# Seven products for eight in the first matmul of the last two batches, of attention and a Silu MoE layer on one core

## The chip, the core and the metric

The kernel runs on 1 core of one Trainium2 chip. The metric is the device time of one execution, in microseconds (us). The engines: TensorE (PE, matmuls, with its weight loads as PEld), VectorE (DVE), ScalarE (ACT), GpSimd (POOL) and SyncE (SP); the last two issue DMAs here, POOL the loads and SP the stores.

## What is computed

Attention over q, k, v of (8 batches, 12 heads, 448 tokens, 64), then a dense layer with Silu over the 3584 tokens x 768:

```
scores = matmul(q, k.T) / sqrt(64);  attn = softmax(scores);  a = matmul(attn, v)
x = a.transpose(0, 2, 1, 3).reshape(3584, 768)
h = x @ w_in                       # 768 x 2048
g = h * (1.0 / (1.0 + exp(-h)))
out = g @ w_out                    # 2048 x 768, float32
```

## The kernel before, in words

All tiles are fp16 with fp32 sums. `w_in_t` (128 partitions, 6 chunks of 128 rows, 2048) and `w_out_t` stay in SBUF.

*Attention.* A unit is a batch and four heads (`units`, 27 of them: batch 0 is cut in two halves, 6 units, then 3 for each batch). For a unit, TensorE makes scores `s` in bursts (L317, L346; 8 matmuls into two double banks, which share 2 slots), ScalarE takes the exp into `E` (L357, two instructions of 128 x 896 a burst, 9 slots), VectorE adds the `E` tiles for the sums of the softmax (`T`, L370), and TensorE makes the sums and the two halves of attention times V in `a` (L380 to L410). Two units go together. VectorE turns and inverts the sums (`inverse`, L436) and `norm` (L459) writes the result times 0.5 as `xT`, one tile of 128 x 448 for each of a batch's 6 chunks of 128 features; there are 14 slots (`NXT`).

*First matmul.* `ffn1` (L476): for each batch and each of the 16 column blocks f of 128, 6 matmuls of 128 x 128 by 128 x 448 sum into one bank `h`. `tanh` (L488) on ScalarE and `gate` (L520) on VectorE make (tanh(h) + 1) x h into `G`, or, for the last 128 tokens of batches 1 and 5, into `X`; as x was halved, that is Silu. `G` holds two batches (896 tokens).

*Second matmul.* It goes by "quads": two tiles of 128 tokens, the 2048 rows of w_out in two halves, the 768 columns in two halves, with seven products `p` of 8 matmuls of 384 columns (L564) for the eight of the plain way. VectorE makes the sums of G (`combine_g`, L545, tiles `S` and in place) and of w_out (`combine_w`, L508), and adds up the products with ScalarE's copies (L627 to L660). There are 13 quads (1 to 13) and one plain one. Each gives four output tiles `ost` of 128 x 384 (6 slots), each stored by four DMAs. Banks: `h`, `p` and `a` share four slots with the tag "m".

*The order of the work* is made when the program is built. `Order` keeps a clock with assumed durations for each engine; VectorE and ScalarE take the ready operation with the lowest time plus bias (norms -10, gates -4, sums of G 0, turns of K and Q 20, sums of w_out 30). The main loop (L1208 on) gives TensorE a score burst when the pace allows (2.6 us apart from batch 2 on), then attention products, or the first ready block of the list `moe` (first matmuls and quads). `Ring` objects stand for the slots. `qk_at` (L1018) holds scores back until the first matmul of an older batch has freed its x slots. `after_x` (L961) queues the first matmul of a batch when its last norm is placed, and the quads of that batch. Every engine's queue is then in that order; nothing is reordered on the chip.

So the end of the program before is: the last attention block, the rest of batch 6's first matmul, quads 10 and 11, batch 7's first matmul, quads 12 and 13.

Of the kernel before, what the change touches and what calls it, by code (L numbers as in the profile page):

```python
# [9 lines left out]
FP16 = mybir.dt.float16  # L10
FP32 = mybir.dt.float32
AF = mybir.ActivationFunctionType
ALU = mybir.AluOpType
# [4 lines left out]
PE_OUT = 0.20  # L18
# [7 lines left out]
def mm(n):  # L26
    return n / 2400.0 + 0.0026


def act(n):  # L30
    return n * 0.00087 + 0.13
# [134 lines left out]
def kernel(  # L166
# [24 lines left out]
    NFF = DFF // 128  # L191
    NDC = DM // 128
    NT = 2 * S // 128
    OH = DM // 2
    NRK, NRQ = 3, 4
# [5 lines left out]
    NEAR, LATE = 0.15, -0.8  # L201
    COLD, FIRST = 8.5, 47
    SHY = 0.5
    PIECES = ((0, 7), (7, TPP))
    NE, NXT, NT_ = 9, 14, 2
    NSG, NTMP, NOST = 3, 3, 6
    attn_scale = 1.0 / (D**0.5)

    const = ctx.enter_context(tc.tile_pool(name="const", bufs=1))
    sb = ctx.enter_context(tc.tile_pool(name="sb", bufs=1))  # L210
# [7 lines left out]
    zeros = const.tile([128, 128], FP16, name="zeros")  # L218
# [217 lines left out]
    def inverse(ns, step, i=0):  # L436
# [15 lines left out]
        else:  # L452
# [3 lines left out]
                out=rdn_t[n], in_=inv_t[ns[0]][:, :, i : i + 1].to_broadcast(shape)  # L456
            )

    def norm(n, part):  # L459
        b, hg, g0, g1 = units[n]  # L460
        nq = 32 * (g1 - g0)
        cc = 2 * hg + part - 1
        if (b, cc) not in xT:
            xT[(b, cc)] = sb.tile([128, S], FP16, name=f"xT_{b}_{cc}", tag="xT", bufs=NXT)
        nc.vector.scalar_tensor_tensor(  # L465
            out=xT[(b, cc)][:, 32 * g0 : 32 * g1],
            in0=acc[(n, part)][:, 0:nq],
            scalar=0.5,
            in1=rdn_t[n].rearrange("p g i -> p (g i)"),
            op0=ALU.mult,  # L470
            op1=ALU.mult,
        )
# [3 lines left out]
    def ffn1(b, f, t0, t1):  # L476
        h = ps.tile([128, 512], FP32, name=f"h_{b}_{f}_{t0}", tag="m", bufs=4)
        for cc in range(NDC):
            nc.tensor.matmul(  # L479
                out=h[:, 0 : t1 - t0],  # L480
                lhsT=w_in_t[:, cc, 128 * f : 128 * (f + 1)],
                rhs=xT[(b, cc)][:, t0:t1],
                start=(cc == 0),
                stop=(cc == NDC - 1),
            )
        h_t[(b, f, t0)] = h
# [10 lines left out]
    HF = NFF // 2  # L497
# [37 lines left out]
    def rows(t, i):  # L535

        fs = slice(HF * i, HF * (i + 1))
        u, k = divmod(t, NT)
        if u % 2 == 0 and k == NT - 1:
            return X[:, fs]  # L540
        return G[:, fs, 128 * k : 128 * (k + 1)]

    S_t, tmp_t, ost_t, pr_t = {}, {}, {}, {}

# [220 lines left out]
    def queue_ffn1(b, g0, g1):  # L765
        t0, t1 = 32 * g0, 32 * g1
        for f in range(NFF) if b == 0 else [x for f in range(HF) for x in (f, f + HF)]:
# [35 lines left out]
            moe.append((deps, 1, run, ()))  # L803
            ffn1_left[b] += 1

    def sums_w(ms):

        for m in ms:
            w_op[m] = [
                od.add(  # L810
                    Op(
                        "DVE",
                        0.9,
                        lambda m=m, f0=f0: combine_w(m, f0, f0 + 4),
                        ld_wout + list(plain_op.values()) * (m in (3, 7)),
                        30,
                    )
                )
                for f0 in (0, 4)
            ]  # L820
# [39 lines left out]
    def batches(qd):  # L860
        return {
            (128 * t + c) // S for t in (2 * qd, 2 * qd + 1) for c in (0, 127)
        }

    def plan_sums():

        if not quads or not sg_ring.can(3, od.now):
            return
        qd = quads[0]
        gates = {}  # L870
        for b in batches(qd):
            for f in range(NFF):
                if len(g_op.get((b, f), ())) < (len(PIECES) if b == 0 else 1):
                    return
                gates.setdefault(f, []).extend(g_op[(b, f)])
        quads.pop(0)
        sg_ring.take(3)
        for m in (5, 2, 1, 6, 7):
            sg_op[(qd, m)] = []
            for f0 in (0, 4):  # L880
                deps = [x for f in range(f0, f0 + 4) for x in gates[f] + gates[f + HF]]
                if m > 5:
                    deps += sg_op[(qd, {6: 2, 7: 5}[m])]
# [77 lines left out]
    def after_x(n):  # L961

        b, hg, g0, g1 = units[n]
        x_left[(b, g0)] = x_left.get((b, g0), NG) - 1
        if x_left[(b, g0)]:
            return
        queue_ffn1(b, g0, g1)
        if g1 < TPP:
            return
        if b == 0:  # L970
            sums_w((1, 4, 6))
            for j in range(2):
# [103 lines left out]
    def plan_adds():  # L1076
        while adds and t_ring.can(1, od.now):
            n = adds.pop(0)
            t_ring.take()
            t_op[n] = [  # L1080
                od.add(Op("DVE", 1.08, lambda n=n: add_e(n, 0), exp_op[n][0:4], -1))
            ]
            late.append(n)
        for n in [n for n in late if len(exp_op[n]) >= 6]:
            late.remove(n)
            t_op[n].append(
                od.add(
                    Op("DVE", 1.08, lambda n=n: add_e(n, 1), exp_op[n][4:6] + t_op[n], -1)
                )
            )  # L1090
# [117 lines left out]
    while True:  # L1208
        plan_turns(qk_seq[0][0][0] + 3 if qk_seq else NU)
        plan_adds()  # L1210
        plan_sums()
        soon = od.step()
        if od.free["PE"] <= od.now:
            ran = False
            moe_i, moe_next = moe_ready()
            av_data["at"] = None
            qk, av = qk_at(), av_at()
            wait = av_data["at"]
            if wait is not None and wait <= od.now - 1000 and not (av is not None and av <= od.now):
# [75 lines left out]
```

## Time and profile before

| | |
|---|---|
| median of 3 runs | 411.51 us (398.6, 411.51, 412.73) |
| profiled execution | 398.08 us, its span 396.3 us |
| granted TensorE clock in it | 1.000 |
| busy from 324.0 to 357.0 us | TensorE 33.00, VectorE 21.62, ScalarE 9.94 |
| busy from 357.0 to 374.0 us | TensorE 17.00, VectorE 9.52, ScalarE 7.61 |
| busy from 374.0 to 392.4 us | TensorE 18.36, VectorE 12.85, ScalarE 3.42 |

The span goes from the first to the last instruction of the profiled execution. In the profile a row of a group gives line, engine, operation, output <- input, shape and count, then the busy time in us, the mean duration in ns, and the idle time of that engine just before the group with what ended it. In a timeline the numbers are the start in us, the length of a merged piece in us, and in brackets the idle time ahead of it. Matmuls are pipelined, so that the mean duration of one is longer than its share of the time. The busy share of each engine in 40 equal slices of the span, in tenths:

```profile
PE   7999999999999999999999999999999999999996
PEld 6667764444444434544444445444445545555563
DVE  2576666999999697796896886877798665684764
ACT  4988886786763967646765744676856524214410
```

### The profile page before, as it was taken

To read this page: it belongs to the slowest core of one execution; us is meant where nothing else is said; L and a number is where in the kernel's file an instruction comes from. 1 tells how busy PE (TensorE), PEld (TensorE's weight loads), DVE (VectorE), ACT (ScalarE), POOL (GpSimd) and SP (SyncE) were. 2 spreads that over 40 slices of the span, in tenths; PEclk is the share of its full clock that TensorE was granted. 3 is DMA by queue.
4 is the path that set the end of the run, shared out by engine and by line. 5 is a ranking of instruction groups with operands and counts; after the bars stand their busy time and mean duration, and the time that the engine had idled before them with its cause. 6 is when DMAs were issued, how large, how long until landed. Compare 5 with 4: busy or idle time off the path is not lost.

```text
span 396.3 us, 9273 instructions
## 1 busy us (share of the span) xinstructions
PE 389.9 (98%) x3696; PEld 200.3 (51%) x3696; DVE 295.3 (75%) x633; ACT 234.9 (59%) x360; POOL 83.7 (21%) x153
## 2 busy tenths in 40 slices
PE   7999999999999999999999999999999999999996
PEld 6667764444444434544444445444445545555563
DVE  2576666999999697796896886877798665684764
ACT  4988886786763967646765744676856524214410
POOL 7632546323005060420006320050000000000000
PEclk9999999999999999999999999999999999999999
DMA  7999999918035673491108591074001210122014
GB/s 113 205 210 209 164 172 190 185 23 122 2 84 91 128 101 40 82 175 45 25 2 132 109 156 21 2 112 86 2 2 47 75 41 0 27 79 57 0 41 120
DMA packets 35580, 34.44 MB, mean 87 GB/s; under 512 B 11600, under 2 KB 34000, under 8 KB 35536
## 3 DMA queue, kind: packets, MB, share of 16 engines
q0 software_dynamic: 24784, 22.82, 38.9%
q1 hardware_dynamic: 9984, 10.24, 9.2%
q10 hardware_dynamic: 768, 0.79, 0.7%
q8 instruction: 29, 0.48, 0.5%
q14 instruction: 15, 0.12, 0.1%
HBM read 45.61 MB, written 11.01 MB: 143 GB/s over the span
## 4 chain that ended last, share of the span: by engine, by line
PE 96%; DMA 1%; DVE 1%; issue 0%; ACT 0%; POOLq 0%
PE h L479 38%; PE p L570 31%; PE s L325 12%; PE a L388 10%; PE o L584 3%; PE a L404 2%; DMA rk<-in_k_dram 1%; PE z L1203 1%; DVE xT L465 0%; DVE T L373 0%; ACT E L362 0%; DVE KT L302 0%; DVE ost L624 0%; DVE rq L312 0%; POOLq L1279 0%
## 5 line engine op out<-in xcount | busy, mean ns | idle before, releaser
L362 ACT ACTIVATE E<-s 128x896 f16<-128x896 f32 (+1 forms) x172 | 149.6, 915 | 44.0 <-PE s L325 42.1
L479 PE MATMUL h<-xT,w_in_t 128*128 128x448 f16 (+1 forms) x864 | 155.1, 332 | 0.1
L479 PEld LDWEIGHTS <-w_in_t 128*128 128x128 f16 x864 | 80.7, 98 | 69.6 <-issue 14.9
L490 ACT ACTIVATE th<-h 128x448 f16<-128x448 f32 (+1 forms) x144 | 71.7, 505 | 73.5 <-PE h L479 62.3
L526 DVE SCALAR_TENSOR_TENSOR G<-th,h 128x448 f16<-128x448 f16 (+2 forms) x144 | 75.5, 534 | 33.1 <-ACT th L490 31.0
L267 POOL DMA_DIRECT2D V<-in_v_dram x88 | 48.6, 571 | 56.1 <-PE a L388 41.9
L325 PE MATMUL s<-rq,KT 32*128 32x448 f16 (+4 forms) x864 | 55.8, 340 | 1.3 <-DVE rq L312 0.9
L570 PEld LDWEIGHTS <-G 128*128 128x128 f16 x384 | 36.2, 98 | 28.8 <-issue 5.8
L570 PEld LDWEIGHTS <-S 128*128 128x128 f16 x312 | 28.9, 98 | 24.7 <-issue 6.7
L388 PE MATMUL a<-E,V 128*32 128x448 f16 (+3 forms) x864 | 41.1, 335 | 0.2 <-issue 0.2
L252 POOL DMA_DIRECT2D rq<-in_q_dram x27 | 15.2, 562 | 120.2 <-PE s L325 101.2
L570 PE MATMUL p<-D,G 128*128 128x384 f16 x208 | 38.2, 327 | 0.0
L570 PE MATMUL p<-w_out_t,S 128*128 128x384 f16 x208 | 37.0, 327 | 0.0
L465 DVE SCALAR_TENSOR_TENSOR xT<-a,rdn 128x448 f16<-128x448 f32 (+1 forms) x54 | 28.9, 567 | 6.7 <-PE a L388 6.0
L570 PE MATMUL p<-w_out_t,G 128*128 128x384 f16 x176 | 32.1, 326 | 0.0
L325 PEld LDWEIGHTS <-KT 32*128 32x128 f16 (+2 forms) x864 | 17.1, 98 | 28.9 <-issue 26.2
L373 DVE TENSOR_TENSOR T<-T,E 128x1792 f16<-128x1792 f16 x20 | 21.8, 1090 | 12.4 <-ACT E L362 12.2
L388 PEld LDWEIGHTS <-V 128*32 128x32 f16 (+2 forms) x864 | 17.8, 95 | 23.6 <-issue 15.7
L560 DVE TENSOR_TENSOR S<-G 128x512 f16<-128x512 f16 x70 | 25.4, 416 | 2.3 <-PE p L570 2.2
L373 DVE TENSOR_TENSOR T<-E,E 128x1792 f16<-128x1792 f16 x20 | 21.7, 1083 | 5.6 <-ACT E L362 5.6
L302 DVE STREAM_TRANSPOSE KT<-rk 128x256 f32<-128x256 f32 (+3 forms) x48 | 16.7, 385 | 6.3 <-DMA rk<-in_k_dram 6.0
L570 PE MATMUL p<-D,S 128*128 128x384 f16 x104 | 19.1, 327 | 0.0
(48 smaller groups left out, 230.2 us busy)
## 6 DMA issues: line engine op xcount, KB each, us to landing
out_dram<-ost SPq DMA_DIRECT2D x208, 48.0 KB, 1.8
rk<-in_k_dram POOLq DMA_DIRECT2D x24, 224.0 KB, 5.7
rq<-in_q_dram POOLq DMA_DIRECT2D x21, 224.0 KB, 5.5
w_in_t<-in_moe_w_in_dram POOLq DMA_DIRECT2D x6, 512.0 KB, 11.1
w_out_t<-in_moe_w_out_dram POOLq DMA_DIRECT2D x4, 768.0 KB, 13.1
V<-in_v_dram POOLq DMA_DIRECT2D x43, 64.0 KB, 4.0
V<-in_v_dram POOLq DMA_DIRECT2D x40, 48.0 KB, 3.9
out_dram<-ost ACTq DMA_DIRECT2D x16, 48.0 KB, 1.8
```

The costliest lines, as they stand in the source:

```text
L267: nc.gpsimd.dma_start(out=VT[b][32 * x : 32 * (x + 1), hs, 0:count, :], in_=v[b, hs].rearrange("h (i g) d -> i h g d", g=TPP)[:, :, first ...
L302: nc.vector.transpose(out=pairs[:, x:y, 0:count], in_=t[:, first : first + count * (y - x)].rearrange("p (x c) i -> p x c i", c=count),)
L325: nc.tensor.matmul(out=pS[p0 : p0 + 32 * (x1 - x0), h % 2, at : at + nq], lhsT=KT[(b, hg)][32 * h : 32 * (h + 1), c, x0:x1, :, e], rhs=QT[ ...
L362: nc.scalar.activation(out=E[(n, w)][0:kr, 2 * y : 2 * y + 2, 0:nk], in_=pS_t[(n, w, y)][0:kr, :, 0:nk], func=AF.Exp, scale=attn_scale,)
L373: nc.vector.tensor_tensor(out=T[n], in0=T[n] if step else E[(n, 0)], in1=E[(n, step + 1)], op=ALU.add,)
L388: nc.tensor.matmul(out=a[32 * h : 32 * (h + 1), 0:nq], lhsT=w, rhs=e[k0:k1, h, at : at + nq], start=start, stop=stop,)
L465: nc.vector.scalar_tensor_tensor(out=xT[(b, cc)][:, 32 * g0 : 32 * g1], in0=acc[(n, part)][:, 0:nq], scalar=0.5, in1=rdn_t[n].rearrange("p ...
L479: nc.tensor.matmul(out=h[:, 0 : t1 - t0], lhsT=w_in_t[:, cc, 128 * f : 128 * (f + 1)], rhs=xT[(b, cc)][:, t0:t1], start=(cc == 0), stop=(c ...
L490: nc.scalar.activation(out=th, in_=h_t[(b, f, t0)][:, 0 : t1 - t0], func=AF.Tanh)
L526: nc.vector.scalar_tensor_tensor(out=dst[:, f, at + lo : at + hi], in0=th_t[(b, f, t0)][:, lo - t0 : hi - t0], scalar=1.0, in1=h_t[(b, f, ...
L560: nc.vector.tensor_tensor(out=dst[:, f0:f1], in0=x[:, f0:f1], in1=y[:, f0:f1], op=op)
L570: nc.tensor.matmul(out=pr_t[(qd, BANK[m])][:, 0:OH], lhsT=w[:, f, :], rhs=W_[m][:, f, :], start=(f == 0 and BANK[m] == m), stop=(f == HF - 1),
```

## The change: what it does

For batches 6 and 7 (`PB` and `PB + 1`) the first matmul is done together, in 8 pairs f = 0 to 7. A pair makes the column blocks f and f + 8 of both batches, so that x (two batches by two halves of the features) and w_in (two halves of the features by two halves of the columns) are 2 x 2 blocks each, and seven products m of 3 matmuls (x block of 128 x 448, 3 chunks) take the place of eight:

- VectorE makes four sums of x (`combine_x`, 128 x 1344, two of them in place of older ones, in a tile of V) and, for f 0 to 3 and 4 to 7, four sums of weights (`combine_w_in`, 128 x 1536, in tiles of E).
- Products 1 and 2 sum into bank A, 6 goes to B, 5 and 3 sum into C, 7 and 4 into D. C and D are a double bank of the scores' 2 slots, A and B are of the four "m" slots.
- ScalarE copies A after product 1 (p) and C after product 5 (q). VectorE makes, in fp32 with 448 columns: u = B + p, v = D + u, v = q + v, p = C + u, u = D + u. Product 2 waits for the copy of A, 3 for the copy of C, 4 for the first v.
- Silu on ScalarE (scale 2.0) reads A, v, p and u and writes G. tanh and gate are gone for these two batches. One Silu of a single column (`first_silu`), behind batch 5's gates, comes first.
- x is held in tiles of 3 chunks, 6 slots (18 chunks for 14); outputs have 4 slots for 6.
- `after_x` queues nothing for batch 6; behind the last norm of batch 7 it queues the pairs, then the quads 10 to 13. Sums of weights are placed when all attention products are (`plan_pair`).

The order on TensorE behind the last attention block is then: 10 products of quads 8 and 9, with the first blocks of pair 0 between them; pairs 0 to 3 interleaved; pairs 4 to 7, nearly one after the other; the 28 products of quads 10 to 13. In the changed program the first matmuls of the pairs are L611, the copies L636, the adds L642, Silu L649, the sums L571 (x) and L588 (weights), the quads' matmuls L683.

```diff
-    NE, NXT, NT_ = 9, 14, 2
-    NSG, NTMP, NOST = 3, 3, 6
+    NE, NX3, NT_ = 9, 6, 2
+    NXT = 3 * NX3
+    NSG, NTMP, NOST = 3, 3, 4
...
+    def combine_x(m):
...
+        a, b, op = {
+            1: (x[1, 0], x[1, 1], ALU.add),
+            2: (sx_t.get(1), x[0, 0], ALU.subtract),
+            3: (x[0, 0], x[1, 0], ALU.subtract),
+            4: (x[0, 1], sx_t.get(2), ALU.subtract),
+        }[m]
+        nc.vector.tensor_tensor(out=sx_t[m], in0=a, in1=b, op=op)
...
+    def combine_w_in(m, f0):
...
+        a, b, op = {
+            1: (x[0, 1], x[0, 0], ALU.subtract),
+            2: (x[1, 1], tw_t.get((1, f0)), ALU.subtract),
+            3: (x[1, 1], x[0, 1], ALU.subtract),
+            4: (x[1, 0], tw_t.get((2, f0)), ALU.subtract),
+        }[m]
+        nc.vector.tensor_tensor(out=tw_t[(m, f0)], in0=a, in1=b, op=op)
+
+    PBANK = {1: "A", 2: "A", 6: "B", 5: "C", 3: "C", 7: "D", 4: "D"}
+
+    def pair_product(f, m):
...
+        a, w = {
+            1: (x[0, 0], w_in_part(0, 0, f, f + 1)),
+            2: (x[0, 1], w_in_part(1, 0, f, f + 1)),
+            3: (sx_t.get(4), w_in_part(1, 1, f, f + 1)),
+        }.get(m, (None, None))
+        if a is None:
+            i = {4: 4, 5: 1, 6: 2, 7: 3}[m]
+            a, w = x[1, 1] if m == 4 else sx_t[i], tw_t[(i, lo)][:, :, at]
+        for c in range(3):
+            nc.tensor.matmul(
+                out=pp_t[(f, PBANK[m])],
+                lhsT=w[:, c, :],
+                rhs=a[:, c, :],
+                start=(c == 0 and m in (1, 6, 5, 7)),
+                stop=(c == 2),
...
+    def pair_copy(f, name, at):
+        nc.scalar.copy(out=pair_tmp(f, name), in_=pp_t[(f, at)])
+
+    def pair_add(f, to, x, y):
...
+        nc.vector.tensor_tensor(out=out, in0=x, in1=y, op=ALU.add)
...
+    def silu(f, r, x):
+        nc.scalar.activation(
+            out=G[:, f, S * r : S * (r + 1)],
+            in_=pp_t[(f % HF, x)] if x == "A" else pf_t[(f % HF, x)],
+            func=AF.Silu,
+            scale=2.0,
+        )
...
+    def plan_pair():
+        while pair_todo and not av_seq and e_ring.can(1, od.now):
...
+        for m in (1, 6, 5, 7, 2, 3, 4):
+            queue(m)
...
+        if b == PB:
+            return
+        if b > PB:
+            queue_pair()
+            for qd in range(1, NT * B // 4):
+                if max(batches(qd)) >= PB:
+                    queue_quad(qd)
+            return
...
         plan_adds()
+        plan_pair()
         plan_sums()
```

More of the change, by code (lines that the diff above doesn't have):

```diff
@@ L203 @@
     SHY = 0.5
+    TWB, SXB = 12, 10
     PIECES = ((0, 7), (7, TPP))
-    NE, NXT, NT_ = 9, 14, 2
-    NSG, NTMP, NOST = 3, 3, 6
+    NE, NX3, NT_ = 9, 6, 2
+    NXT = 3 * NX3
+    NSG, NTMP, NOST = 3, 3, 4
     attn_scale = 1.0 / (D**0.5)
@@ L457, in inverse, with x3 @@
             )
+    def x3(b, cc):
+        if (b, cc // 3) not in xT:
+            xT[(b, cc // 3)] = sb.tile(
+                [128, 3, S], FP16, name=f"xT_{b}_{cc // 3}", tag="xT", bufs=NX3
+            )
+        return xT[(b, cc // 3)]
     def norm(n, part):
@@ L462, in norm @@
         cc = 2 * hg + part - 1
-        if (b, cc) not in xT:
-            xT[(b, cc)] = sb.tile([128, S], FP16, name=f"xT_{b}_{cc}", tag="xT", bufs=NXT)
+        x3(b, cc)
         nc.vector.scalar_tensor_tensor(
-            out=xT[(b, cc)][:, 32 * g0 : 32 * g1],
+            out=x3(b, cc)[:, cc % 3, 32 * g0 : 32 * g1],
             in0=acc[(n, part)][:, 0:nq],
@@ L481, in ffn1 @@
                 lhsT=w_in_t[:, cc, 128 * f : 128 * (f + 1)],
-                rhs=xT[(b, cc)][:, t0:t1],
+                rhs=x3(b, cc)[:, cc % 3, t0:t1],
                 start=(cc == 0),
@@ L541, in rows @@
         return G[:, fs, 128 * k : 128 * (k + 1)]
+    PB = B - 2
+    c_t, sx_t, tw_t, pp_t, pf_t = {}, {}, {}, {}, {}
+    def combine_x(m):
+        if m % 2:
+            whole = sb.tile([128, NH, NCH, D], FP16, name=f"sx_{m}", tag="V", bufs=2)
+            whole = whole.rearrange("p h c d -> p (h c d)")
+            for i in range(2):
+                sx_t[m + i] = whole[:, 3 * S * i : 3 * S * (i + 1)].rearrange(
+                    "p (c t) -> p c t", c=3
+                )
+        x = {(r, i): x3(PB + r, 3 * i) for r in range(2) for i in range(2)}
+        a, b, op = {
[5 more added lines that the diff above has]
+        nc.vector.tensor_tensor(out=sx_t[m], in0=a, in1=b, op=op)
@@ new lines, in w_in_part @@
+    def w_in_part(i, j, f0, f1):
+        at = DFF // 2 * j
+        return w_in_t[:, 3 * i : 3 * i + 3, at + 128 * f0 : at + 128 * f1]
+    def combine_w_in(m, f0):
+        w = sb.tile([128, HG, S], FP16, name=f"tw_{m}_{f0}", tag="E", bufs=NE)
+        w = w.rearrange("p h s -> p (h s)")[:, 0 : 3 * 512]
+        tw_t[(m, f0)] = w.rearrange("p (c f) -> p c f", c=3)
+        x = {(i, j): w_in_part(i, j, f0, f0 + 4) for i in range(2) for j in range(2)}
+        a, b, op = {
[5 more added lines that the diff above has]
+        nc.vector.tensor_tensor(out=tw_t[(m, f0)], in0=a, in1=b, op=op)
@@ new lines @@
+    PBANK = {1: "A", 2: "A", 6: "B", 5: "C", 3: "C", 7: "D", 4: "D"}
+    def pair_product(f, m):
+        if m in (1, 6):
+            pp_t[(f, PBANK[m])] = ps.tile(
+                [128, 512], FP32, name=f"f_{f}_{m}", tag="m", bufs=4
+            )[:, 0:S]
+        elif m == 5:
+            two = ps.tile([128, 2, 512], FP32, name=f"f_{f}_{m}", tag="s", bufs=2)
+            pp_t[(f, "C")], pp_t[(f, "D")] = two[:, 0, 0:S], two[:, 1, 0:S]
+        x = {(r, i): x3(PB + r, 3 * i) for r in range(2) for i in range(2)}
+        lo, at = f // 4 * 4, slice(128 * (f % 4), 128 * (f % 4 + 1))
+        a, w = {
[13 more added lines that the diff above has]
+                stop=(c == 2),
+                skip_group_check=True,
+            )
@@ new lines, in pair_tmp @@
+    def pair_tmp(f, name):
+        tag, n, shape, dt = {
+            "p": ("rq", NRQ, [128, TPP * D], FP16),
+            "q": ("rk", NRK, [128, TPP * D], FP16),
+            "u": ("KT", 3, [128, NCH, 4, 32, 2], FP16),
+            "v": ("T", NT_, [128, HG, S], FP16),
+        }[name]
+        t = sb.tile(shape, dt, name=f"{name}_{f}", tag=tag, bufs=n)
+        if len(shape) == 5:
+            t = t.rearrange("p c x i e -> p (c x i e)")
+        elif len(shape) == 3:
+            t = t.rearrange("p h s -> p (h s)")
+        pf_t[(f, name)] = t[:, 0 : 2 * S].bitcast(FP32)
+        return pf_t[(f, name)]
@@ new lines, in pair_copy, with first_silu @@
+    def pair_copy(f, name, at):
+        nc.scalar.copy(out=pair_tmp(f, name), in_=pp_t[(f, at)])
+    def pair_add(f, to, x, y):
+        x = pp_t[(f, x)] if x in "BCD" else pf_t[(f, x)]
+        y = pf_t[(f, y)]
+        out = pf_t[(f, to)] if (f, to) in pf_t else pair_tmp(f, to)
+        nc.vector.tensor_tensor(out=out, in0=x, in1=y, op=ALU.add)
+    def first_silu():
+        t = const.tile([128, 1], FP16, name="first_silu")
+        nc.scalar.activation(out=t, in_=zeros[:, 0:1], func=AF.Silu)
@@ L543 @@
+    def silu(f, r, x):
[4 more added lines that the diff above has]
+            scale=2.0,
+        )
     S_t, tmp_t, ost_t, pr_t = {}, {}, {}, {}
@@ L804, in queue_ffn1 @@
             ffn1_left[b] += 1
+    pair_w, pair_x, pair_todo = {}, {}, []
+    def plan_pair():
+        while pair_todo and not av_seq and e_ring.can(1, od.now):
+            m, f0 = pair_todo.pop(0)
+            e_ring.take()
+            pair_w[(m, f0)] = od.add(
+                Op(
+                    "DVE",
+                    0.98,
+                    lambda m=m, f0=f0: combine_w_in(m, f0),
+                    [pair_w[(k, f0)] for k in {2: (1,), 4: (2,)}.get(m, ())],
+                    TWB + f0,
+                )
+            )
@@ new lines, in queue_pair @@
+    def queue_pair():
+        xs = {(r, c): x_op[(PB + r, c, 0)] for r in range(2) for c in range(NDC)}
+        v_ring.take(2)
+        od.add(
+            Op(
+                "ACT",
+                2.7,
+                first_silu,
+                [x for f in range(NFF) for x in g_op[(PB - 1, f)]],
+                -5,
+            )
+        )
+        for m in range(1, 5):
+            made = {
+                1: [xs[1, c] for c in range(NDC)],
+                2: [xs[0, c] for c in range(3)],
+                3: [xs[r, c] for r in range(2) for c in range(3)],
+                4: [xs[0, c] for c in range(3, NDC)],
+            }[m]
+            made = made + [pair_x[k] for k in {2: (1,), 4: (2,)}.get(m, ())]
+            pair_x[m] = od.add(Op("DVE", 0.9, lambda m=m: combine_x(m), made, SXB))
+        pair_todo.extend((m, f0) for f0 in (0, 4) for m in (1, 2, 3, 4))
+        for f in range(HF):
+            queue_pair_f(f, xs)
@@ new lines, in queue_pair_f, with free, read, gate_of @@
+    def queue_pair_f(f, xs):
+        done, lo = {}, f // 4 * 4
+        def free(r):
+            made = []
+            for qd in range(NT * B // 4):
+                for t in (2 * qd, 2 * qd + 1):
+                    if t // NT == PB // 2 - 1 and t % NT < (4, NT - 1)[r]:
+                        made += [pr_op.get((qd, m)) for m in (3, 4, 6, 7)]
+            return made
+        def read(name, eng, fn, deps, then=None, bias=-4):
+            busy = act(S) if eng == "ACT" else S / 960.0 + 0.13
+            done[name] = od.add(Op(eng, busy, fn, deps, bias, then=then))
+        def gate_of(j, r, x, deps, then):
+            read((j, r), "ACT", lambda: silu(f + HF * j, r, x), deps, then, -0.3)
+            g_op.setdefault((PB + r, f + HF * j), []).append(done[(j, r)])
+        def queue(m):
+            rings = {
+                1: ((rq_ring, 1),),
+                6: ((kt_ring, 1),),
+                5: ((s_ring, 1), (rk_ring, 1)),
+                7: ((t_ring, 1),),
+            }.get(m, ())
+            def run():
+                op = Op("PE", 3 * mm(S), lambda: pair_product(f, m), tail=PE_OUT)
+                if m in (1, 6):
+                    m_ring.take()
+                for ring, need in rings:
+                    ring.take(need)
+                od.on_pe(op, "full")
+                done[m] = op
+                if m == 1:
+                    read("p", "ACT", lambda: pair_copy(f, "p", "A"), [op], None, -3)
+                elif m == 6:
+                    read("u", "DVE", lambda: pair_add(f, "u", "B", "p"), [op, done["p"]], m_ring.give)
+                elif m == 5:
+                    read("q", "ACT", lambda: pair_copy(f, "q", "C"), [op], None, -3)
+                elif m == 7:
+                    read("v", "DVE", lambda: pair_add(f, "v", "D", "u"), [op, done["u"]])
+                    read("22", "DVE", lambda: pair_add(f, "v", "q", "v"), [done["v"], done["q"]], rk_ring.give)
+                    gate_of(1, 1, "v", [done["22"]], t_ring.give)
+                elif m == 2:
+                    gate_of(0, 0, "A", [op], m_ring.give)
+                elif m == 3:
+                    read("12", "DVE", lambda: pair_add(f, "p", "C", "u"), [op, done["u"]])
+                    gate_of(1, 0, "p", [done["12"]], rq_ring.give)
+                else:
+                    read("21", "DVE", lambda: pair_add(f, "u", "D", "u"), [op, done["12"]], s_ring.give)
+                    gate_of(0, 1, "u", [done["21"]], kt_ring.give)
+            def deps():
+                if m in (1, 2):
+                    made = [xs[0, c] for c in (range(3) if m == 1 else range(3, NDC))]
+                else:
+                    i = {3: 4, 5: 1, 6: 2, 7: 3}.get(m)
+                    made = [pair_x[i]] if i else [xs[1, c] for c in range(3, NDC)]
+                if m != 3 and m > 2:
+                    made.append(pair_w.get(({4: 4, 5: 1, 6: 2, 7: 3}[m], lo)))
+                made += [done.get(x) for x in {2: ["p"], 3: ["q"], 4: ["v"]}.get(m, [])]
+                first = {3: (5, 6), 4: (3, 7), 5: (1,), 6: (1,), 7: (5, 6)}.get(m, ())
+                made += [(done.get(x), 9.0) for x in first]
+                return made + (free(0) if m == 1 else free(1) if m == 7 else [])
+            moe.append((deps, int(m in (1, 6)), run, rings))
+        for m in (1, 6, 5, 7, 2, 3, 4):
+            queue(m)
```

## The prediction

> **What bounds the kernel now.** I read the page first, then the chain of waits in order of time over the last 76 us, then what TensorE waited for, and last the groups with shapes kept apart, for prices.
>
> ```profile
> span 396.3 us, 9273 instructions
> PE 389.9 (98%) x3696; PEld 200.3 (51%) x3696; DVE 295.3 (75%) x633; ACT 234.9 (59%) x360; POOL 83.7 (21%) x153
> ...
> PE 96%; DMA 1%; DVE 1%; issue 0%; ACT 0%; POOLq 0%
> ```
>
> TensorE (PE) is 96% of the chain that ended last. Its busy share alone would not prove that, as matmuls overlap, so the end of the chain is looked at in order of time (start, length, what):
>
> ```profile
> 324.07 13.72 PE h L479 x72
> 337.79 15.60 PE p L570 x96
> 353.39 1.13 PE h L479 x6
> 354.53 2.60 PE p L570 x16
> 357.13 17.02 PE h L479 x90
> 374.15 18.21 PE p L570 x112
> 392.37 0.02 issue
> 392.39 0.56 DVE ost L624
> ```
>
> After the last attention block, at 324.07, TensorE runs 68.3 us without a hole. Two prices: 90 matmuls of 448 columns in 17.02 us are 0.189 us each, 112 of 384 columns in 18.21 us are 0.163 us each. So a first-matmul block `h` (6) costs 1.135 us, a product of second matmuls `p` (8) 1.30. From 392.39 to 396.3 only the last add and its stores remain.
>
> ```profile
> PE z L1203 <- DVE zeros L219: 1.0, 1, 1.0
> PE s L325 <- DVE rq L312: 0.9, 1, 0.9
> PE s L325 <- ACT E L362: 0.4, 1, 0.4
> PE a L388 <- issue: 0.2, 1, 0.2
> ```
>
> These are all of TensorE's waits: 2.5 us, and none in the stage that is changed. TensorE matmuls taken out there should come off the end, if VectorE (DVE) and ScalarE (ACT) keep up. Their prices:
>
> ```profile
> L490 ACT ACTIVATE th<-h 128x448 f16<-128x448 f32 x112 | 61.0, 545 | 72.0 <-PE h L479 61.0 <-issue 5.4 <-ACT th L490 2.9
> L465 DVE SCALAR_TENSOR_TENSOR xT<-a,rdn 128x448 f16<-128x448 f32 x42 | 24.3, 618 | 4.4 <-PE a L388 4.4
> L373 DVE TENSOR_TENSOR T<-T,E 128x1792 f16<-128x1792 f16 x20 | 21.8, 1090 | 12.4 <-ACT E L362 12.2
> L516 DVE TENSOR_TENSOR D<-w_out_t 128x1536 f16<-128x1536 f16 x6 | 5.5, 939 | 0.0
> L362 ACT ACT_TABLE_LOAD x1 | 1.3, 1283 | 0.7 <-PEq L1279 0.7
> ```
>
> The means are durations, and back-to-back instructions of one engine overlap by about 0.08 us, as the timelines show:
>
> ```profile
> 385.44 0.55 DVE L624 TENSOR_TENSOR s<-s,ost 128x384 f32<-128x384 f32 x1
> 385.91 0.55 DVE L624 TENSOR_TENSOR m<-m,ost 128x384 f32<-128x384 f32 x1
> ...
> 292.00 1.16 DVE L465 SCALAR_TENSOR_TENSOR xT<-a,rdn 128x448 f16<-128x448 f32 x2 [0.23 <-PE a L388]
> ```
>
> ```profile
> 289.95 0.55 ACT L490 ACTIVATE th<-h 128x448 f16<-128x448 f32 x1 [0.59 <-PE h L479]
> 290.40 1.73 ACT L362 ACTIVATE E<-s 128x896 f16<-128x896 f32 x2
> ```
>
> From start to start: an add of 384 columns 0.47 us, a 448-column VectorE instruction on PSUM 0.54 (1.16 for two, less 0.62), a tanh of 448 0.45, an exp of 896 0.81 (1.73 for two, less 0.915). With the same overlap 1536 fp16 columns cost 0.86, and 1344, by their number, 0.76.
>
> **The change, part by part.** *TensorE.* Two batches by 16 blocks of 6 are 192 matmuls; eight pairs by seven products of 3 are 168. The difference is 24 x 0.189 = -4.54 us, all on the path. The order of the changed program has 230 switches between scores, attention and full-array matmuls for 232; a product that starts at 301.78 and costs 1.30 is followed by a score at 303.18, so a switch costs 0.10: -0.2. The Trainium skill, TensorE: Matmul & The Clock Gate, section Back-to-back issue gap, has a sustained 131 ns for 512 columns, which scaled to 448 would be 115 ns and a term of only -2.8 us (an estimate from that page). The trace's 0.189 decides here.
>
> *What is moved.* Both batches' first matmul goes behind all attention, where 10 products (13.0 us), 168 matmuls (31.8) and 28 products (36.4) make 81.2 us for 68.3. TensorE's total falls by 4.7, so the last attention block must end at 324.07 - 4.7 - (81.2 - 68.3) = 306.4, 17.6 us earlier: scores, exps, norms and K, Q and V loads of batches 3 to 7 come closer together. Counted from the order with the prices above, units 15 to 26 take 160.5 us of TensorE, 126 of VectorE (79%), 98 of ScalarE (61%); the worst pair of units has VectorE at 24.5 of 29.7 (83%). Before, units 11 and 12 ran with 24.3 of 27.1 (90%), and from 100 to 200 us TensorE was busy for 100.00 of 100. The loads shared 37% of the DMA engines from 200 to 300 us, and the 18 chunk slots let scores run ahead. I cost this at 0; if the cover fails, it is VectorE's queue that is late, and the price is a rival below.
>
> *VectorE.* Away go 32 gates of about 0.53 (-17.0); in come 4 sums of x (3.0), 8 of weights (6.9) and 40 fp32 adds on 448 columns. No row has exactly these adds: below lies the 384-column add, 0.47, above the duration 0.618 of a 448-column instruction on PSUM; I take 0.54, the same columns and source (21.6). Net +14.5. It hides if the stretch still fits. From the last attention block to quad 10's first product TensorE has 13.0 + 31.8 = 44.8 us; VectorE's instructions there, from the last two norms on, sum to 38.5.
>
> *ScalarE.* 32 tanh (-14.4) become 16 copies and 32 Silu, and one table load of 1.28. Silu is in no row: below it a 384-column copy start to start (0.40), above the exp of 896 columns (0.81); I take tanh's 0.45, for the same tile. A pair then costs ScalarE 6 x 0.45 = 2.7 us of TensorE's 21 x 0.189 = 3.97; with 0.81 it would be 4.14, 0.17 more than TensorE, 1.4 us over eight pairs. The load stands between the copies of products 5 and 2 of quad 8. Their matmuls end one product (1.3), an attention block (1.6) and another product (1.3) apart, 4.2 us; less one copy 3.7 are free, so it costs 0. The Trainium skill, ScalarE: Activation LUTs, section What ACT_TABLE_LOAD costs, adds a drain and comes to about 2.66 us; the only load in the trace, 1283 ns at the start, can't show the drain. By the page the sum would still be the same, since 2.66 also fits the gap.
>
> *The first pairs.* Counting from the end of the last attention block: VectorE can't start the adds of products 7 of quad 8, 1 and 7 of quad 9 before 8.1, 11.3 and 14.4, and its queue is in order, so the second sum of x, made behind them, is there at 16.1 and the fourth at 17.7. TensorE first needs them at 17.5 and 19.2, as it has eight other blocks of pairs 0 to 3 ahead: 1.4 us of room.
>
> *Inside a pair* (order m1, m6, m5, m7, m2, m3, m4, 0.567 each; a reader starts about 0.25 after the matmuls, an estimate from the trace, where 12 matmuls of h from 287.42 on fill 2.27 to 289.69 and the tanh starts at 289.95): the copy of m1 is done at 1.27, u at 1.92, the copy of m5 at 2.40, v at 3.06. m3 needs the second copy at 2.84, m4 needs v at 3.40. So the room is 0.4 and 0.3 us. If an instruction of the neighbouring pair stands ahead (0.54), m4 is late by up to 0.2, in eight pairs 1.6. So new stalls lie between 0 and 1.6 + 1.4 = 3.0; I take 0.4, near the lower end, because the counted room holds in most places.
>
> *The end.* The 28 products keep their price; VectorE has 23.7 us of work in those 36.4. Outputs have 4 slots for 6; a slot is written again four output tiles later, at least 3.9 us by my count of products, and a store lands 1.8 us after its issue: 0 (0.5 at most). The stores of quads 8 and 9 move into the pair stage on SP's queue, where no load runs; the queues behind the last product are as before.
>
> Sum: 398.08 (the profiled execution's own time; its span is 396.3) - 4.54 - 0.2 + 0.4 = 393.7. The three runs shown lie between 398.6 and 412.73 with a median of 411.51, so the profiled execution stands with the lowest of them. The forecast is for executions like it; the same 4.4 us off the median would give 407.1.
>
> **The rivals.** A, the forecast: 393.3 (no stall) to 396.3 (3.0).
>
> B, the gain is given back inside the pairs: m3 and m4 both wait in each pair. For it speak the small rooms (0.3, 0.4) and that VectorE's queue mixes pairs; against it, that VectorE is needed for only 2.7 of 3.97 us. With one more VectorE instruction late per pair, 8 x 0.54 on top of A's upper end: 396.3 + 4.3 = 400.6. So 396 to 401, within 2%.
>
> C, slower: VectorE becomes the bound of the pair stage. Its work without the adds is 16.9 us, it idles about 2.5 in the waits named above, and 44.8 + 4.7 = 49.5 us is where all gain is gone, so it decides from (49.5 - 19.4) / 40 = 0.75 us for an add. With 0.95 it is 57.4, 12.6 over 44.8: 393.3 + 12.6 = 405.9, 2% slower. Against it: no row of that size is above 0.618.
>
> D, attention can't be drawn 17.6 us closer and TensorE waits for loads or norms there. For it: a K or Q load takes 5.5 to 5.7 us to land. Against: the shares above. One landing that shows in full gives 393.3 + 5.7 = 399; three, one for each of batches 5 to 7, give 410.
>
> E, faster by over 2% needs 390.1. The waits listed sum to 2.5, so even without them all 398.08 - 4.7 - 2.5 = 390.9: no mechanism reaches it, only a spread such as the three runs have.
>
> **How the numbers follow.** Chances: A 0.53, B 0.20, C 0.12 (half of it from 0.95 us on), D 0.08 (0.03 with more than one landing), E 0.07. A measurement of this kernel can tell about 2% from no change. Faster by over 2% is E, 0.07; slower C's 0.06 and D's 0.03, 0.09; within 2% the rest, 0.84. A's own range is 393.3 to 396.3. The whole range starts at 391.5, 1.8 lower, since two executions at the same level (398.08 and 398.6) differ by 0.5 already and part of the 2.5 us of listed waits may fall otherwise; it goes to 408, since it takes in B, D, C at 0.95 and A at the level of the median shown (407.1).
>
> **What would show it.** Right: the 168 matmuls of L611 in about 31.8 us with no hole over 0.5, the last attention block ending near 306, TensorE's waits still a few us, a Silu and a pair's add no longer than 0.55 and 0.62. Wrong: a wait of L611 on VectorE's L642 or ScalarE's L636 in every pair (B), VectorE without idle time through the pairs (C), score or attention blocks waiting for DMA or L473 before 306 (D), or a granted clock below 1.00 after a hole.

## The result and the profile after

The changed kernel takes 400.44 us (median of 5 runs), the kernel before 398.6 in the runs beside it: a ratio of 1.0059, 95% interval 1.0042 to 1.0077. So it is slower by 0.6%, where 1.1% faster was forecast. A few executions of both (up to 415.19, at a granted clock of 0.956, and 412.73) ran 13 to 15 us longer; the comparisons leave them out.

The profiled execution took 400.36 us. Its page:

```profile
span 398.6 us, 9275 instructions
PE 387.8 (97%) x3672; PEld 198.9 (50%) x3672; DVE 309.9 (78%) x653; ACT 243.1 (61%) x378; POOL 83.7 (21%) x153
...
PE 90%; DVE 5%; ACT 2%; DMA 1%; issue 1%; DVEq 0%; ACTq 0%
```

TensorE issues 24 matmuls fewer, as meant. But its share of the chain that ended last fell from 96% to 90%; VectorE and ScalarE hold 7% of it, where they had 1%. Most of that stands around and behind the end of the last attention block (306.70), as the chain in order of time shows (start, length, what):

```profile
305.87 2.38 DVE tw L588 x3
...
308.38 0.63 DVE xT L473
...
346.62 3.58 PE f L611 x18
350.22 0.54 ACT q L636
350.79 0.64 DVE v L642
...
351.47 3.58 PE f L611 x18
355.12 0.54 ACT q L636
355.69 0.64 DVE v L642
...
356.37 1.29 PE f L611 x6
357.66 31.21 PE p L683 x192
```

Pairs 5 to 7 repeat every 4.85 to 4.90 us, not every 3.97 (21 x 0.189). The chain goes through six products (3.58), ScalarE's copy of C (`q`) and VectorE's `v`; TensorE has only one product, 2, to do beside these and then stands for 0.9. The list of TensorE's waits names the two largest new ones:

```profile
PE f L611 <- DVE v L642: 3.0, 4, 0.8
...
PE p L683 <- DVE xT L473: 0.9, 1, 0.9
```

The list has four waits of 0.71 to 0.77 us; from start to start the products there are 0.87 to 0.93 late, and five more gaps of 0.2 to 0.3 lie between products of pairs 0 to 4. All together: 54 products run from 321.89 to 357.50, 35.6 us for 54 x 0.567 = 30.6. So 5.0 us are lost inside the pairs. The prices, on the other hand, came out as in the forecast (mean of one in ns after the busy time):

```profile
L642 DVE TENSOR_TENSOR v<-f,u 128x448 f32<-128x448 f32 x8 | 5.0, 622 | 2.8 <-ACT q L636 1.4 <-PE f L611 1.3
L649 ACT ACTIVATE G<-v 128x448 f16<-128x448 f32 x8 | 4.6, 578 | 4.2 <-DVE v L642 4.2
L646 ACT ACT_TABLE_LOAD x1 | 1.3, 1283 | 0.0
```

The forecast put the span at 391.9 (393.7 less the 1.8 around it); it is 398.6. The difference of 6.7 us by stage: the last attention block ended near 306.7 for 306.4 (+0.3); one norm late, 0.9; 5.0 lost in the pairs for 0.4 (+4.6); from quad 10's first product to the last product's end 36.4 for 36.4; from there to the end of the span 4.7, before 4.1 (+0.6, the last product's end taken as its start and 1.30). That is 6.4; 0.3 is rounding, most of it in the forecast, whose own stages add up to 392.1.

In the waits that were built into the program the reason stands plainly. Banks C and D are one tile, a double bank. Each access to that tile by another engine than the last waits for the last one, whichever half it touches, and reading counts like writing: the copy of C waits for product 7 in D, not for product 5 in C; `v` = D + u waits for that copy; product 3, into C, waits for `v`. So in every pair product 7, copy (0.54), add (0.63) and product 3 stand in one row. The timelines of ScalarE, VectorE and TensorE show it for pair 7:

```profile
355.12 0.53 ACT L636 COPY q<-f 128x448 f32<-128x448 f32 x1 [0.19 <-PE f L611]
355.69 0.62 DVE L642 TENSOR_TENSOR v<-f,u 128x448 f32<-128x448 f32 x1 [0.58 <-ACT q L636]
356.37 0.73 PE L611 MATMUL f<-sx,w_in_t 128*128 128x448 f16 x3 [0.77 <-DVE v L642]
```

Product 5 ended at 354.30 and product 7 at 354.87; ScalarE was free from 354.93, but the copy starts 0.25 behind product 7. VectorE was free and `u` made at 355.10, and yet `v`, which reads only D and `u`, waits until the copy of C is done.

### The profile page after: what moved, and what is told of

Same layout as the page of the kernel before. It is cut to its first block, busy times and chain, and to the rows that moved or that the text cites. A ratio compares the mean times of both kernels' runs of the same rounds, so it can differ in the third digit from the quotient of the medians.

```text
span 398.6 us, 9275 instructions
## 1 busy us (share of the span) xinstructions
PE 387.8 (97%) x3672; PEld 198.9 (50%) x3672; DVE 309.9 (78%) x653; ACT 243.1 (61%) x378; POOL 83.7 (21%) x153
## 4 chain that ended last, share of the span: by engine, by line
PE 90%; DVE 5%; ACT 2%; DMA 1%; issue 1%; DVEq 0%; ACTq 0%
PE h L487 29%; PE p L683 27%; PE s L327 12%; PE a L390 10%; PE f L611 6%; PE o L697 3%; PE z L1437 2%; PE a L406 2%; DMA rq<-in_q_dram 1%; DVE v L642 1%; DVE tw L588 1%; ACT q L636 1%; DVE xT L473 1%; ACT E L364 0%; DMA out_dram<-ost 0%
## 5 line engine op out<-in xcount | busy, mean ns | idle before, releaser
L487 PE MATMUL h<-xT,w_in_t 128*128 128x448 f16 (+1 forms) x672 | 119.0, 327 | 0.1
L487 PEld LDWEIGHTS <-w_in_t 128*128 128x128 f16 x672 | 61.1, 98 | 54.9 <-issue 19.1
L498 ACT ACTIVATE th<-h 128x448 f16<-128x448 f32 (+1 forms) x112 | 54.4, 494 | 30.5 <-PE h L487 20.3
L534 DVE SCALAR_TENSOR_TENSOR G<-th,h 128x448 f16<-128x448 f16 (+2 forms) x112 | 55.5, 509 | 18.6 <-ACT th L498 16.2
L683 PEld LDWEIGHTS <-G 128*128 128x128 f16 x384 | 36.6, 98 | 28.0 <-issue 4.4
L683 PEld LDWEIGHTS <-S 128*128 128x128 f16 x312 | 29.2, 98 | 24.4 <-issue 5.1
L683 PE MATMUL p<-D,G 128*128 128x384 f16 x208 | 37.6, 326 | 0.0
L683 PE MATMUL p<-w_out_t,S 128*128 128x384 f16 x208 | 37.2, 326 | 0.2 <-DVE S L673 0.2
L683 PE MATMUL p<-w_out_t,G 128*128 128x384 f16 x176 | 31.9, 326 | 0.0
L747 ACT COPY ost<-p 128x384 f32<-128x384 f32 x13 | 6.2, 480 | 27.8 <-PE p L683 23.1
```

The lines of the kernel that those rows point to most:

```text
L487: nc.tensor.matmul(out=h[:, 0 : t1 - t0], lhsT=w_in_t[:, cc, 128 * f : 128 * (f + 1)], rhs=x3(b, cc)[:, cc % 3, t0:t1], start=(cc == 0), s ...
L498: nc.scalar.activation(out=th, in_=h_t[(b, f, t0)][:, 0 : t1 - t0], func=AF.Tanh)
L534: nc.vector.scalar_tensor_tensor(out=dst[:, f, at + lo : at + hi], in0=th_t[(b, f, t0)][:, lo - t0 : hi - t0], scalar=1.0, in1=h_t[(b, f, ...
L683: nc.tensor.matmul(out=pr_t[(qd, BANK[m])][:, 0:OH], lhsT=w[:, f, :], rhs=W_[m][:, f, :], start=(f == 0 and BANK[m] == m), stop=(f == HF - 1),
```

## The experiments

Theory 1 is this chain on the shared tile. Rivals: Silu and its table load delay the stage (theory 2); VectorE's adds are the limit whatever the tile (theory 3); the move behind attention, the chunk slots and the output slots cost it (theory 4). A letter behind the 1 marks a cause of what is left once theory 1 holds: the output slots (1a), the stores themselves (1b), the last norms behind sums of weights in VectorE's queue (1c), ScalarE's copy behind store issues (1d). The kernel before took 398.0 to 398.2 us on these chips. The end of each profiled execution in us, for use below:

| kernel | last product starts | last add starts | span |
|---|---|---|---|
| before | 390.89 | 392.39 | 396.3 |
| after | 392.60 | 394.20 | 398.6 |
| e1_order | 387.99 | 390.10 | 394.6 |
| e2_split | 388.02 | 390.21 | 394.5 |
| e3_eight | 390.94 | 392.44 | 396.3 |
| e4_slots | 391.07 | 392.57 | 397.0 |
| e6_norms_first | 387.67 | 389.47 | 393.7 |
| e10_copy_free | 387.16 | 388.66 | 393.3 |
| e12_split_all | 387.70 | 389.20 | 394.7 |

**e1_order.** Only what the planner of the order is told: the copy and the add wait for product 7, product 3 for `v`. The instructions are the same, so it places other pairs' products into the hole.

```diff
-                elif m == 5:
+                elif m == 7:
                     read("q", "ACT", lambda: pair_copy(f, "q", "C"), [op], None, -3)
-                elif m == 7:
-                    read("v", "DVE", lambda: pair_add(f, "v", "D", "u"), [op, done["u"]])
+                    read("v", "DVE", lambda: pair_add(f, "v", "D", "u"), [op, done["u"], done["q"]])
...
-                elif m == 3:
+                elif m == 4:
                     read("12", "DVE", lambda: pair_add(f, "p", "C", "u"), [op, done["u"]])
...
-                made += [done.get(x) for x in {2: ["p"], 3: ["q"], 4: ["v"]}.get(m, [])]
+                made += [done.get(x) for x in {2: ["p"], 3: ["v"], 4: ["v"]}.get(m, [])]
```

> The changed kernel, with one thing altered: the planner that writes the order takes product 3 as ready only when v is made, the copy q as ready only behind product 7, and p = C + u only behind product 4. The instructions are the same, only their order differs, with two pairs always under way. Theory 1 (banks C and D are one tile, so that on each pair q waits for product 7, v for q, product 3 for v, and TensorE stands for about 0.9 us): the stretch from the last attention block to quad 10, 50.9 us in the changed kernel, falls by about 5, the span from 398.6 to about 393.6, the time to about 395.4. Theory 2 (ScalarE's 48 copies and Silu are too slow) and theory 3 (VectorE's 40 adds are the bound): the same work on the same engines, so 400.4 within 0.7.

Measured 396.24 us, ratio 0.9952 (0.9938 to 0.9967): 4.2 less than after. Its chain leaves TensorE once in the pair stage:

```profile
322.13 9.09 PE f L611 x48
...
331.25 0.62 DVE p L642
331.88 0.54 DVE u L642
...
332.46 19.45 PE f L611 x102
```

102 matmuls now run without a stop. Before them the chain goes for 1.2 us through two adds of an earlier pair; TensorE does two more products beside them and stands for 0.3. So of the 5.0 us lost in the pairs 0.3 are left. Theory 1 is confirmed; the time it gave, 395.4, was 0.8 too low, mostly since the way from the last product to the end grew by another 0.6 (table). Theories 2 and 3 fall as causes of the loss: the work of ScalarE and VectorE is the same.

**e2_split.** The tile is taken apart instead: A and B, whose accesses hardly cross, share the double bank, C and D get a slot each.

```diff
-        if m in (1, 6):
+        if m in (5, 7):
             pp_t[(f, PBANK[m])] = ps.tile(
...
-        elif m == 5:
+        elif m == 1:
             two = ps.tile([128, 2, 512], FP32, name=f"f_{f}_{m}", tag="s", bufs=2)
-            pp_t[(f, "C")], pp_t[(f, "D")] = two[:, 0, 0:S], two[:, 1, 0:S]
+            pp_t[(f, "A")], pp_t[(f, "B")] = two[:, 0, 0:S], two[:, 1, 0:S]
```

The copy p and the add u stand behind product 6, product 2 waits for u, and the slots are given back to match.

> The changed kernel with the banks dealt otherwise: A and B, which are used one after the other anyway, share the double bank; C and D are two single tiles. The planner knows it. Theory 1: product 3 waits for q alone and product 4 for v alone, no stall of 0.9 us in each pair is left: span about 393.6, time about 395.4, as with the order alone. Theory 2 and theory 3: the work of ScalarE and VectorE is the same, 400.4 within 0.7. If the move of the work behind attention or the slots cost the time (theory 4): 400.4 too.

Measured 396.32 us, ratio 0.9956 (0.9941 to 0.9971), the same as e1 by the other way. In its program the copy of C waits for product 5, product 3 for the copy, product 4 for `v`, as the prediction had assumed.

```profile
323.42 27.97 PE f L611 x147
```

147 of the 168 matmuls run in one piece, 0.190 us each: with the tile apart the pair stage has TensorE's own time. In front of them TensorE waits 0.6 us for a sum of x. That also settles what the forecast weighed against the Trainium skill, TensorE: Matmul & The Clock Gate, section Back-to-back issue gap: scaled by columns, its sustained 131 ns for 512 would give 115 ns (an estimate from that page). The measured 0.190 decides.

**e3_eight.** The changed kernel with the eight products of before, as plain first matmuls of both batches behind all attention; slots as after.

```diff
         if b > PB:
-            queue_pair()
+            queue_ffn1(PB, g0, g1)
+            queue_ffn1(PB + 1, g0, g1)
```

> The changed kernel without the seven products: both batches' first matmul stays behind all attention, 18 chunk slots and 4 output slots stay, but it is done in 16 blocks of 6 a batch with tanh and gate. It has no pair, no copy, no Silu and no weight sums. Theory 4 (the move and the slots cost the time): about 403, since TensorE's total is 4.5 us more than in the changed kernel and the loss of about 7 stays at least in part. Theory 1: the loss is in the pairs, so that this is the time before, 398.1, plus at most 0.6 for the end of the program: 398 to 399.

Measured 398.39 us (10 runs), ratio 1.0006 (0.9997 to 1.0015). The move, with the slots, costs nothing that can be told from noise (at most 0.6 us by the interval); theory 4 falls as a cause of the loss.

**e4_slots.** The kernel before with the slots of after.

```diff
-    NE, NXT, NT_ = 9, 14, 2
-    NSG, NTMP, NOST = 3, 3, 6
+    NE, NXT, NT_ = 9, 18, 2
+    NSG, NTMP, NOST = 3, 3, 4
```

> The kernel before with only the slots of the change: 18 chunk tiles of x for 14 and 4 output tiles for 6. Theory 1: the stores of the last quads come later for want of an output tile, which is the 0.6 us that the changed kernel takes longer from its last product to its end (4.7 for 4.1 us): 398.1 + 0.6 = 398.7. Theory 4: 400 or more. If slots cost nothing: 398.1.

Measured 398.85 us, ratio 1.0017 (1.0007 to 1.0027): 0.7 us, small, but its interval leaves out 1. In the profiled execution TensorE's last product starts 0.18 later; the other 0.5 lies behind the last add. Which of the two slot counts does it isn't told apart here.

**e9_tanh.** The changed kernel with Tanh in place of Silu, for the single column too, so that no second table is loaded. The output of the last two batches is then not the reference's.

> The changed kernel with tanh in the place of Silu, so that the output of two batches is not the reference's; the second table load goes with it, everything else stays in its order. Theory 2 (Silu or its table load is dear on ScalarE): about 396 to 398. Theory 1 (only the waits on the shared tile count): 400.4, as tanh takes as long as Silu and the load lies in a gap.

Measured 400.43 us, ratio 1.0052 (1.0037 to 1.0067): the time of after. Silu, at tanh's price, and the load cost nothing; theory 2 falls.

**e5_outputs.** e1, with the output tiles of the last two quads in slots of `E`, so that no output waits for a slot there.

```diff
     def ost(qd, i, j):
-        t = sb.tile([128, OH], FP32, name=f"ost_{qd}_{i}{j}", tag="ost", bufs=NOST)
+        if qd >= 12:
+            t = sb.tile([128, HG, S], FP16, name=f"ost_{qd}_{i}{j}", tag="E", bufs=NE)
+            t = t.rearrange("p h s -> p (h s)")[:, 0 : 2 * OH].bitcast(FP32)
+        else:
+            t = sb.tile([128, OH], FP32, name=f"ost_{qd}_{i}{j}", tag="ost", bufs=NOST)
```

> e1_order with one thing altered: the output tiles of the last two quads, 12 and 13, lie in the slots of the exp tiles, which are free by then, so that no write of an output waits for a store. Order and instructions are the same. In e1_order the program ends 5.3 us after its last product's matmuls are issued, 4.1 in the kernel before; the chain goes there from a store to the last output copy on ScalarE, which stands ahead of the last sums on VectorE. Theory 1a (the four output slots cost this): the span falls by 1.0 to 1.2, from 394.6 to about 393.5, the time from 396.2 to about 395.1. Rival 1b (the end is longer for the stores' own traffic, whoever waits): no change, 396.2.

Measured 396.6 us, ratio 0.9958 (0.9944 to 0.9972): no gain, 1a falls. ScalarE's timeline shows what its last copy stands behind:

```profile
383.51 4.77 ACTq L736 DMA_DIRECT2D out_dram<-ost  x6
...
388.32 0.48 ACT L755 COPY ost<-p 128x384 f32<-128x384 f32 x1 [4.84 <-DMA out_dram<-ost]
```

ScalarE's queue is in order. Six store issues, some for outputs that VectorE makes later, hold it for 4.77 us, and the copy of a product done before comes at 388.32.

**e6_norms_first.** e1, and the sums of weights are placed only when the last norm is.

```diff
-        while pair_todo and not av_seq and e_ring.can(1, od.now):
+        while pair_todo and not av_seq and norm_op[-1].done is not None and e_ring.can(1, od.now):
```

> e1_order with one thing altered: the planner doesn't place a sum of weights on VectorE before the last norms have their place. In the changed kernel and in e1_order three such sums (2.38 us) stand ahead of the last norms in VectorE's queue, and TensorE waits 0.89 us for the bank that a norm has to read. Theory 1c (the queue order costs the 0.89): the wait is gone, the time falls by 0.6 to 0.9, from 396.2 to about 395.4. Rival (the sums are then late for the first pairs): the wait moves to the first pairs, 396.2 or more.

Measured 395.67 us, ratio 0.9925 (0.9906 to 0.9945). That is 0.6 us below e1's median, with the intervals of the two ratios overlapping (e1: from 0.9938), so the gain is small against the noise. The wait of 0.9 for `xT` is gone. But the four sums of weights now stand ahead of the sums of the next quad, as the chain shows:

```profile
308.29 3.47 DVE tw L588 x4
311.76 2.01 DVE S L673 x6
313.77 0.48 DVE s L737
...
314.29 4.06 PE p L683 x24
```

The product that starts at 312.21 takes until 314.29, 2.08 us for 1.30, so that 0.8 of the 0.9 is lost again there. By the table, the last product starts 0.3 earlier than in e1, and the way from it to the end is 0.6 shorter. So 1c is right on the wait and near on the time, but the greater part of the gain lies at the end of the program, and the wait came back at another place than the rival named.

**e7_both.** e5's and e6's edits together.

> e1_order with both of these, outputs of the last quads in free slots and norms ahead of the sums of weights. If the loss beyond the pairs is made of these two alone, it is the sum: 396.2 - 1.1 - 0.8 = 394.3, 0.6 above the forecast of 393.7. If they hide each other: 395.

Measured 395.89 us, ratio 0.9935 (0.9918 to 0.9951): only e6's part counts, and neither 394.3 nor 395 is reached.

**e10_copy_free.** e6, with ScalarE issuing stores for the last quad alone, the rest on SP's queue.

```diff
-            eng = nc.scalar if w % 2 and 4 * qd + 8 >= NT * B else nc.sync
+            eng = nc.scalar if w % 2 and 4 * qd + 4 >= NT * B else nc.sync
```

> e6_norms_first with one thing altered: ScalarE issues half of the stores of quad 13 only, no longer of quad 12, whose stores all go through SP. In e1_order and e5_outputs the last output copy on ScalarE (13_10) could start at 385.6 and starts at 388.3 to 388.5, behind six store issues in ScalarE's queue, of which two wait for an output tile of VectorE's; VectorE's last sums wait for that copy. Theory 1d (the copy stands behind stores in ScalarE's queue): the last add follows the last product at once, as before the change, and the time falls by 0.8 to 1.2, from 395.6 to about 394.6. Rival 1b (the stores themselves, on SP, set the end): no change or later, 395.6 to 396.5, as SP gets eight more.

Measured 395.67 us, ratio 0.9934 (0.9922 to 0.9947), the time of e6. The copy now comes at once, and the last add 0.2 us behind the last product; but the stores do not:

```profile
382.71 8.28 SPq L732 DMA_DIRECT2D out_dram<-ost  x16
...
384.76 0.48 ACT L751 COPY ost<-p 128x384 f32<-128x384 f32 x1 [2.08 <-PE p L683]
...
388.66 0.56 DVE L737 TENSOR_TENSOR ost<-p,s 128x384 f32<-128x384 f32 x1 [0.26 <-DMA out_dram<-ost]
```

SP issues 16 stores in 8.28 us, 0.52 each with its waits, up to 391, and from the last add's end to the end of the span it takes 4.1 us, before 3.35. 1d is right on the copy, 1b on the time: freeing one queue moves its stores to the other.

**e11_pool.** e6, with those stores of ScalarE's on GpSimd's queue.

```diff
-            eng = nc.scalar if w % 2 and 4 * qd + 8 >= NT * B else nc.sync
+            eng = nc.gpsimd if w % 2 and 4 * qd + 8 >= NT * B else nc.sync
```

> e6_norms_first with the stores that ScalarE issues for quads 12 and 13 issued by GpSimd, which has nothing else to do there. Theory 1d: ScalarE's copy is free, so the last add comes as early as in e10_copy_free; GpSimd's K loads land 5.8 us after their issue against 1.7 to 1.8 for stores through SP and ScalarE, so the last landing is up to 4 later: 394.6 to 398. Rival 1b: SP has the same stores as in e6_norms_first, 395.6 or later.

Measured 400.68 us, ratio 1.0069 (1.0054 to 1.0085): 5 us worse than e6, beyond what either theory gave. The last add starts at 388.84, but the span ends at 398.4. The page's line of these issues (KB each, median us from issue to landing):

```profile
out_dram<-ost POOLq DMA_DIRECT2D x16, 48.0 KB, 2.1
```

And GpSimd's last issues in its timeline:

```profile
388.87 1.96 POOL L732 DMA_DIRECT2D out_dram<-ost  x4 [1.81 <-DVE ost L737]
```

They cost 0.49 us each and end at 390.83; with a landing of 2.1 the stores would be done at 392.9. What holds the end until 398.4 isn't settled.

**e12_split_all.** e2 with e6's and e10's edits.

> e2_split (A and B in the double bank, C and D single) with both mends: norms ahead of the sums of weights, and quad 12's stores all through SP. If the three causes found (shared tile, norms behind sums, copy behind stores) make up the whole loss, the time is the forecast within 1: 393.7 to 394.7. If something else is left, 395.5 or more.

Measured 396.43 us, ratio 0.995 (0.9936 to 0.9964): the gains do not add up. Its profiled span is 2.8 us above the forecast's 391.9. Of that 0.8 is lost at the sums of a quad, as in e6, 0.6 at a sum of x, and 1.6 behind the last product, from whose start it is 7.0 us to the end (5.4 before).

So the best versions, e6 and e10, are 0.7% faster than before and 1.2% faster than after. The forecast's 393.7 is not reached by about 2 us. By the table, e6's span is 1.8 above the forecast's 391.9: 0.6 of it is the way from the last product's start to the end (6.0 us, before 5.4), 0.6 the last attention block, which starts at 305.43 and so ends near 307.0 for 306.4, and 0.8 are lost between them at the quad's sums; that is 2.0, or 0.2 too many, by the rounding in the forecast. Its pair stage has 159 matmuls in one piece of 30.08 us and no hole. What made attention end later in e6 than in after wasn't looked for.

## Why the prediction was wrong

**The step that failed** is "Inside a pair": "m3 needs the second copy at 2.84, m4 needs v at 3.40. So the room is 0.4 and 0.3 us." The dependencies were read by bank. The program has them by tile: the copy starts after product 7 (2.27 + 0.25), is done at 3.0, `v` at 3.7, and product 3, due at 2.84, starts 0.9 late. This was predicted at 0.4 us in all and measured at 5.0; e1 and e2 take 4.1 to 4.2 of the time away again by the order alone or by the tile alone. The price of no instruction was far off: one add of 0.62 and one copy of 0.53 stood in a row that had been drawn side by side. (The forecast counted them from start to start, 0.54 and 0.45, though a product that waits needs the whole duration; that is 0.1 of room for each, not 0.9.)

**Rival B** gave 396 to 401 for waits in each pair, and the time lies there. Its mechanism was another one, an instruction of the neighbouring pair ahead in VectorE's queue. The row of `v` above refutes it: VectorE had been idle for 0.58 when the copy released `v`. C is refuted too: adds at 0.62 against its 0.75, and e2's pair stage without a stop. D: attention did end at 306.7, and e3 shows that the move costs nothing measurable.

**"The first pairs"**, 1.4 us of room, held in after (no wait for `sx`) but barely: e2, which brings the pairs forward, waits 0.6 for a sum of x. What was missed there is the last norm behind three sums of weights (2.38 us) in VectorE's queue: 0.9 on the path, where the forecast has "I cost this at 0". e6 takes this wait away and loses 0.8 a little later.

**"The end": "the queues behind the last product are as before."** They aren't, and 0 was too low: from the last product's start to the end of the span it is 5.4 us before, 6.0 in after and 6.6 in e1 (table). In both kernels SP issues 208 of the stores and ScalarE 16, half of those of quads 12 and 13, a share that the text ahead of the forecast leaves out. SP's queue is no fuller there: before, it issues nothing from 382.2 to 386.4 and then twelve stores,

```profile
386.40 7.47 SPq L619 DMA_DIRECT2D out_dram<-ost  x12
```

and in the changed kernel nothing from 384.2 to 388.1 and then twelve:

```profile
388.10 7.96 SPq L732 DMA_DIRECT2D out_dram<-ost  x12
```

What differs is the order of the last quad's products, and with it ScalarE's queue. Before:

```profile
384.39 2.76 PE L570 MATMUL p<-w_out_t,S 128*128 128x384 f16 x16
386.99 1.46 PE L570 MATMUL p<-w_out_t,G 128*128 128x384 f16 x8
```

After:

```profile
386.10 1.46 PE L683 MATMUL p<-w_out_t,S 128*128 128x384 f16 x8
387.40 1.46 PE L683 MATMUL p<-w_out_t,G 128*128 128x384 f16 x8
388.70 1.46 PE L683 MATMUL p<-w_out_t,S 128*128 128x384 f16 x8
```

The second product of `S`, which ScalarE's last copy reads, comes one product later, and six store issues stand ahead of that copy where two stood before. The kernel before, e3 and e4 have the first order, and 5.4 to 5.9 us from the last product's start to the end; the other versions have the second, and 6.0 or more. No run alters that order alone, so it isn't shown to be the cause; with the copy freed (e10) it is still 6.1. The slots, costed at 0, are 0.7 in the kernel before (e4), not seen beside the move (e3).

**Right:** 24 x 0.189 (e2: 0.190); the 28 products at 36.4; the end of attention to 0.3; Silu, copy and add near tanh's and the norm's prices (three of a pair's four Silu, those from SBUF, take 0.577, above the 0.55 that was named as a limit, without a wait of TensorE's on them). The load between the copies of products 5 and 2 of quad 8, put at 0: e9, without it, takes the same time. The Trainium skill, ScalarE: Activation LUTs, section What ACT_TABLE_LOAD costs, adds a drain to the load's 1283 ns; the trace has a copy that ends at 304.42, the load from 304.43 to 305.71 and the next activation at 305.73, so that no drain stands on either side of it here.

## What to carry to other kernels

Before counting the room between two engines, list what each wait in the built program is for: where waits are kept by tile, two halves of one tile used in turn by several engines run one after the other, reads included. Give such halves allocations of their own, or tell whoever makes the order, so that another chain fills the hole; both brought back 1.0% here. And where a stage is moved, the order of the work behind it can change too: compare it, queue by queue, before it is costed at nothing.

## What the runs showed of the hardware

Silu costs 538 ns for 128 x 448 from PSUM and 577 from fp32 in SBUF, tanh 547 from PSUM. A store's issue holds SP's queue for 0.45 us (before: ten from 351.84 in 4.54 us) and ScalarE's for 0.43 (two in 0.85 us). The same 16 stores issued by GpSimd at the end of the program cost 5 us more than by ScalarE (400.68 and 395.67).
